# A fused attention and gated linear unit on one core: the order of all tasks from a table, squares and mean in one VectorE step

## The chip, the cores and the metric

The kernel runs on one core of a Trainium2 chip. A core has several engines, each with its own queue of instructions, which it works off in order: TensorE (PE in the profile) multiplies matrices, VectorE (DVE), ScalarE (ACT) and GpSimd (POOL) work on elements, and SyncE (SP) issues the transfers (DMA). The engines wait for each other by semaphores. Matrices are multiplied out of the on-chip memory SBUF into PSUM, which has eight banks of 128 x 512 float32.

The metric is the device time of one execution in microseconds, lower is better. The kernel before takes 272.04 us (median of three runs, 271.98 to 272.32).

## The reference

Attention with a feature map and no softmax (4 batches, 4 heads, 1088 positions, 32 wide), and behind it a normalised gated linear unit on the 4352 rows of 128:

```python
def phi(x):                                   # S1, S2: 8 x 32
    a = einsum('rd,bhsd->bhsr', S1, x); b = einsum('rd,bhsd->bhsr', S2, x)
    return einsum('bhsi,bhsj->bhsij', a, b).reshape(..., 64)
kv = einsum('bhsf,bhsd->bhfd', phi(k), v);  z = phi(k).sum(over s)
x  = (phi(q) @ kv) / (phi(q) . z + 1e-06)     # then heads side by side: 4352 x 128

xn  = x / sqrt(mean(x * x, -1) + 1e-06) * rms_g
out = (silu(xn @ w_gate) * (xn @ w_val)) @ w_out     # 128 -> 1536 -> 128
```

S1, S2 and the weights come as float64.

## The kernel before

**Attention.** For each batch, `kside` loads the transposed keys (`kt`) and the values (`vt`), multiplies the keys by S1 and S2 (L570, result in a PSUM bank), makes the 64 products per head (`product`, L531 on DVE or L513 on POOL, into `phi`), and sums `phi` times values over the positions (L580) into `kv`. The 4352 queries are worked in nine chunks, eight of 512 and one of 256. For chunks 0 and 1, `qside` makes the products in natural layout (L624, L531, `phn`) and transposes them (L632). For the others it multiplies first (L651, `sab`), stores the halves to memory (`far`) and reads them back spread out (`at`, `bt`); L677 multiplies them. Then come the numerator and denominator (L693), the division (L711, L712, L703), the squares (L715 on ACT, with the sum over the row written by the same instruction's accumulator), mean plus epsilon (L725 on DVE), the power of -1/2 (L728 on POOL), `xn` (L731 or L749), its transposes (L735), and `x_hi` and `x_lo`.

**Weights.** The float64 words of one of 12 slices of the weights, `w_raw` (384 KB), are turned into float32 on DVE in five steps of 128 x 384 (L426 or, on ACT, L445; L429, L433, L437, L440), then split into a high part `w_hi` (ACT, L494) and the rest `w_lo` (L497, DVE or POOL).

**The gated unit.** A slot is one chunk with one slice, 108 in all. Its gate goes to a bank `g_ps` and its value to a bank `v_ps`, each with three matmuls in a fast format, high by high, high by low, low by high (L786). ACT takes the silu (`s`, L795), DVE multiplies (`h`, L798), ACT rounds it to `h_hi` (L813), DVE takes the rest `h_lo` (L816), and three more matmuls add to the chunk's output in `o_ps` (L822). The first four and the last two slots use one float32 matmul instead (L805). There are two banks each of `g_ps` and `v_ps`, one `o_ps`, three `att`; four buffers of `h` and five each of `h_hi` and `h_lo`. The slots of chunks 0 and 1 are taken in halves of six slices, so that each slice of the weights serves two chunks.

**What sets the order.** None of this is issued where it stands in the code. Each step is given to a planner (`Plan.add`) as a task with its possible engines and their lengths, what it reads and writes, and its buffers. `Plan.forward` then walks a model of the engines: among the tasks that could start, it takes the one with the smallest `late`, a due time out of a table with one number per task (`LATE`), decides the engine by which would end first, and emits the instructions sorted by the modelled start. Where the model shows PE idle, small matmuls on zeros are put in (`keep_warm`, L420), the fillers. The instruction order on each engine is then fixed by dependencies.

Of the kernel before, what the change touches and what calls it, by code (L numbers as in the profile page):

```python
# [912 lines left out]
```

## Time and profile before

| what | value |
|---|---|
| median of the runs | 272.04 us |
| the profiled execution | 272.2 us |
| its span, first to last instruction | 270.0 us |
| PE busy | 263.7 us (98%) |
| DVE busy | 201.0 us (74%) |
| ACT busy | 162.1 us (60%) |
| POOL busy | 23.2 us (9%) |
| read from memory, written | 18.69 MB, 3.08 MB |

The span is shorter than the execution's time by what lies before the first and behind the last instruction. In rows of the order of time the columns are start, length, engine, line, operation, output and inputs with shapes and count, and in brackets the idle time before and what ended it. Lengths of successive instructions on one engine overlap, so that the cost of one in a stream is the distance from its start to the next. In rows of groups they are the sum of the lengths and the mean in ns, then the engine's idle time ahead of the group. Plain float32 matmuls appear as two instructions each. In rows by stretch they are the busy time of PE, the weight load, DVE, ACT and POOL, then the granted clock of TensorE, the share of the transfer engines, and GB/s.

### The profile page before, as it was taken

The page shows a single profiled execution, that of the slowest core. Times are in us where ns is not written, and L with a number is a line of the kernel's source. Part 1 is how long each engine was busy: PE and PEld are TensorE (multiplying, and loading weights), DVE is VectorE, ACT ScalarE, POOL GpSimd, SP SyncE. Part 2 cuts the span into 40 slices and gives each one's busy share as a digit, 9 for nine tenths or more (in the row PEclk, how much of TensorE's full clock was granted, in tenths as well). Part 3 has the DMA queues.
Part 4 walks back from the last instruction along what each step waited for, and adds up shares of the span by engine and source line. Part 5 has one row for each costly group of instructions (what it writes and reads, how often), then busy time and mean ns, then how long its engine had stood idle before and what let it go on. Part 6 is the DMA issues. An engine that isn't in the chain of part 4 may idle for free.

```text
span 270.0 us, 4975 instructions
## 1 busy us (share of the span) xinstructions
PE 263.7 (98%) x1842; PEld 209.4 (78%) x1842; DVE 201.0 (74%) x383; ACT 162.1 (60%) x385; POOL 23.2 (9%) x37
## 2 busy tenths in 40 slices
PE   7899999999999999999999999999999999999995
PEld 4767687687788787778778787887777887887895
DVE  3799999999676786659646967678757755967582
ACT  4488796557554665717587556546646553855671
POOL 3132221230100010000100010001000100000000
PEclk9999999999999999999999999999999999999999
DMA  6999333041045001520016101610042001200100
GB/s 201 395 401 353 105 92 83 0 128 55 2 123 170 4 0 47 129 79 2 0 58 161 35 1 40 165 34 0 10 131 75 0 0 50 81 0 0 41 0 19
DMA packets 12087, 22.08 MB, mean 82 GB/s; under 512 B 1568, under 2 KB 3360, under 8 KB 12064
## 3 DMA queue, kind: packets, MB, share of 16 engines
q1 hardware_dynamic: 11920, 21.78, 25.5%
q8 instruction: 14, 0.23, 0.3%
q14 instruction: 9, 0.07, 0.1%
q10 hardware_dynamic: 144, 0.00, 0.0%
HBM read 18.69 MB, written 3.08 MB: 81 GB/s over the span
## 4 chain that ended last, share of the span: by engine, by line
PE 90%; DVE 4%; DMA 2%; ACT 1%; SPq 1%; issue 1%; POOL 0%; ACTq 0%
PE g_ps L786 26%; PE v_ps L786 26%; PE o_ps L822 24%; PE att L693 3%; PE att L580 3%; DMA vt<-v 2%; PE o_ps L805 2%; PE att L735 1%; PE att L651 1%; PE att L570 1%; PE o_ps L580 1%; DVE h L798 1%; DVE w_tmp L433 1%; DVE h_lo L816 0%; ACT h_hi L813 0%
## 5 line engine op out<-in xcount | busy, mean ns | idle before, releaser
L798 DVE TENSOR_TENSOR h<-v_ps,s 128x512 f32<-128x512 f32 (+2 forms) x109 | 70.1, 654 | 32.8 <-ACT s L795 16.1
L795 ACT ACTIVATE s<-g_ps 128x512 f32<-128x512 f32 (+1 forms) x108 | 60.2, 572 | 38.9 <-PE g_ps L786 21.6
L813 ACT CAST h_hi<-h 128x512 fp32r<-128x512 f32 (+1 forms) x102 | 59.5, 598 | 27.1 <-DVE h L798 23.0
L816 DVE TENSOR_TENSOR h_lo<-h,h_hi 128x512 fp32r<-128x512 f32 (+1 forms) x102 | 66.3, 667 | 10.4 <-ACT h_hi L813 9.0
L786 PE MATMUL g_ps<-x_hi,w_hi 128*128 128x512 f32 (+2 forms) x111 | 43.2, 389 | 0.0
L786 PE MATMUL v_ps<-x_hi,w_hi 128*128 128x512 f32 (+2 forms) x111 | 42.7, 384 | 0.0
L786 PE MATMUL g_ps<-x_hi,w_lo 128*128 128x512 f32 (+2 forms) x111 | 41.9, 378 | 0.4 <-DVE w_lo L497 0.4
L786 PE MATMUL v_ps<-x_lo,w_hi 128*128 128x512 f32 (+2 forms) x111 | 42.0, 378 | 0.0
L786 PE MATMUL v_ps<-x_hi,w_lo 128*128 128x512 f32 (+2 forms) x111 | 41.8, 377 | 0.0
L786 PE MATMUL g_ps<-x_lo,w_hi 128*128 128x512 f32 (+2 forms) x111 | 41.8, 378 | 0.0
L822 PE MATMUL o_ps<-h_hi,w_hi 128*128 128x512 f32 (+1 forms) x102 | 40.1, 393 | 0.0
L822 PE MATMUL o_ps<-h_lo,w_hi 128*128 128x512 f32 (+1 forms) x102 | 39.1, 383 | 0.0
L822 PE MATMUL o_ps<-h_hi,w_lo 128*128 128x512 f32 (+1 forms) x102 | 39.1, 383 | 0.0
L728 POOL TENSOR_TENSOR rstd<-ms,mhalf 128x4 f32<-128x4 f32 (+1 forms) x10 | 10.0, 1000 | 187.6 <-DVE ms L725 187.6
L786 PEld LDWEIGHTS g_ps<-x_hi,w_hi 128*128 128x128 f32 x111 | 20.9, 188 | 5.3 <-ACT s L795 0.6
L786 PEld LDWEIGHTS v_ps<-x_hi,w_hi 128*128 128x128 f32 x111 | 20.9, 188 | 4.6 <-DVE h L798 0.3
L786 PEld LDWEIGHTS g_ps<-x_hi,w_lo 128*128 128x128 f32 x111 | 20.9, 188 | 4.4 <-DVE w_lo L497 0.8
L786 PEld LDWEIGHTS v_ps<-x_lo,w_hi 128*128 128x128 f32 x111 | 20.9, 188 | 4.2
L786 PEld LDWEIGHTS g_ps<-x_lo,w_hi 128*128 128x128 f32 x111 | 20.8, 188 | 4.2
L786 PEld LDWEIGHTS v_ps<-x_hi,w_lo 128*128 128x128 f32 x111 | 20.9, 188 | 3.9
L822 PEld LDWEIGHTS o_ps<-h_hi,w_hi 128*128 128x128 f32 x102 | 19.2, 188 | 5.5 <-issue 1.3
L822 PEld LDWEIGHTS o_ps<-h_lo,w_hi 128*128 128x128 f32 x102 | 19.2, 188 | 4.1
(85 smaller groups left out, 257.8 us busy)
## 6 DMA issues: line engine op xcount, KB each, us to landing
w_raw<-w SPq DMA_DIRECT2D x12, 384.0 KB
bt<-far SPq DMA_DIRECT2D x24, 128.0 KB
at<-far SPq DMA_DIRECT2D x12, 256.0 KB
q<-qT SPq DMA_DIRECT2D x8, 256.0 KB
outT<-o_sb SPq DMA_DIRECT2D x8, 256.0 KB
vt<-v SPq DMA_DIRECT2D x4, 340.0 KB
kt<-kT SPq DMA_DIRECT2D x4, 320.0 KB
vt<-v SPq DMA_DIRECT2D x4, 272.0 KB
```

The source lines that it names most:

```text
L433: nc.vector.tensor_scalar(out=u, in0=u, scalar1=5, scalar2=2, op0=ALU.logical_shift_left, op1=ALU.logical_shift_right)
L570: nc.tensor.matmul(out=ab()[hf * HALF:(hf + 1) * HALF, (t - lo) * HALF:(t - lo + 1) * HALF], lhsT=kt()[:, s0:s0 + HALF], rhs=sblk, start=T ...
L580: nc.tensor.matmul(out=kvv[rows, h // 2, :], lhsT=phi()[:, t, h * F:(h + 1) * F], rhs=vt()[:, t, h, :], start=(t == 0 and h < 2), stop=(t ...
L693: nc.tensor.matmul(out=nv[hf * HALF:(hf + 1) * HALF, t, p, :], lhsT=phi()[:, p, l0:l0 + HALF], rhs=kvs[(s0 + l0) // S][:, p, :], start=Tru ...
L728: nc.gpsimd.tensor_tensor(out=rstd()[:, us, 0], in0=ms()[:, us], in1=mhalf[:, us], op=ALU.pow)
L786: nc.tensor.matmul(out=acc()[:, cs], lhsT=wt[:, j, i3, :], rhs=x()[:, cs], start=(i == 0), stop=(i == 2))
L795: act(n, lambda: nc.scalar.activation(out=s()[:, :n], in_=gps()[:, :n], func=AF.Silu), cols(gps, whole[0]), [s])
L798: cs.stop - cs.start, lambda cs=cs: nc.vector.tensor_tensor(out=h()[:, cs], in0=vps()[:, cs], in1=s()[:, cs], op=ALU.mult),
L805: (cs.stop - cs.start) * 1.69, lambda cs=cs: nc.tensor.matmul(out=o_ps()[:, cs], lhsT=w_f[:, j, 2], rhs=h()[:, cs], start=first, stop=last ...
L813: act(n, lambda: nc.scalar.copy(out=h_hi()[:, :n], in_=h()[:, :n]), hs, [h_hi], True)
L816: eng.tensor_tensor(out=h_lo()[:, :n], in0=h()[:, :n], in1=h_hi().bitcast(F32)[:, :n], op=ALU.subtract)
L822: nc.tensor.matmul(out=o_ps()[:, :n], lhsT=wt[:, j, 2, :], rhs=x()[:, :n], start=first and i == 0, stop=last and i == 2,)
```

## The change

**The order.** `LATE` and the planner's choice are replaced by two tables: `ORDER`, the list of all 1252 tasks in the order in which they are placed, and `ON`, one letter for each task that has more than one possible engine. `Plan.follow` only computes modelled starts along that list, for the fillers and for the order in which instructions of different engines are emitted.

**Engines.** More tasks have a choice: the 64 products of keys and natural queries and those of the other chunks (`phi`, `phn`, `phiq`) on DVE or POOL, `h_lo` on DVE or POOL, plain copies on ACT or DVE. By the table, 48 of 102 `h_lo`, seven `phiq` and four `phi` or `phn` now are POOL's, and DVE has four output copies that were ACT's. The copy ahead of a product now takes both factors, not one.

**The norm.** The squares leave ACT: one DVE instruction multiplies, scales by 1/128, adds up and adds epsilon; L715 and L725 go, and L588 comes, 34 times, each with its accumulator read. The norm's weights come as a last column of batch 0's keys, in place of a transfer of their own on ACT's queue; ACT copies the column (L415).

**Loads.** The first slice of the weights is loaded first, the first queries in two halves, and batch 0's values in three pieces.

```diff
-LATE = """
--37035 -1206 -8314 1298 -10490 18870 15192 16396 -27501 -26844 -12692 -5713 -5435 -16853 4745 -3012 -1650 -18178 12804 -4772 -6470 -36037 -1883 12817
...
+ORDER = """
+67 68 69 70 11 0 12 1 4 2 3 5 6 39 40 8 34 16 71 66 72 20 35 9 41 13 205 21 7 22 210 73 77 17 36 42 14 18 211 24 15 28 75 25 206 297 74 37 207 212 26
...
+ON = (
+    "apadadaddaapaadaaadppappadpappappaddapdadpdppadpaddadpadddadddapaadaaddaapaddddaapdadddpdpadddddddppddpddddadadapdadddpp"
...
+    def follow(self, clock0, filler):
...
+            t.on = {"a": "act", "d": "dve", "p": "pool"}[next(many)] if len(t.ways) > 1 else next(iter(t.ways))
+        for i in map(int, ORDER.split()):
+            t = self.tasks[i]
...
     def product(out, ab, m, writes):
+        both = sb("both", [P, 4 * H, 2, R], 3)
...
+        copy(m * HALF, lambda: both()[:, :m * H], view, [ab], [both])
+        plan.add({
+            "dve": on_dve(m * H * F, lambda: outer(nc.vector, view())),
+            "pool": on_pool(m * H * F * 0.85, lambda: outer(nc.gpsimd, both()[:, :m * H]), PHI_POOL),
+        }, [ab, both], writes)
...
-            cs = slice(lo * P, hi * P)
+            cs = slice(lo * P, hi * P + (first and hi == KT))
...
+            act(1, lambda: nc.scalar.copy(out=gain_t, in_=kt()[:, SP:]), [(kt, 1)], ["gain"], True)
...
-                plan.add({"act": Way(300, 400, lambda t=t, u=u, sq=sq: nc.scalar.activation(
-                    out=sq()[:, t], in_=x()[:, u + t], func=AF.Square, accum_out=ss()[:, u + t:u + t + 1]
-                ))}, [(x, u)], [(sq, t), (ss, u + t)])
+                def mean(t=t, u=u, sq=sq):
+                    nc.vector.tensor_tensor_reduce(
+                        out=sq()[:, t], in0=x()[:, u + t], in1=x()[:, u + t], scale=1.0 / DM, scalar=EPS, op0=ALU.mult, op1=ALU.add,
+                        accum_out=ms()[:, u + t:u + t + 1],
+                    )
+
+                plan.add({"dve": Way(265, 345, mean, True)}, [(x, u)], [(sq, t), (ms, u + t)])
...
-            dve(n, lambda: low(nc.vector), [*hs, h_hi], [h_lo], lock=True)
+            plan.add({
+                "dve": on_dve(n, lambda: low(nc.vector), True), "pool": on_pool(n, lambda: low(nc.gpsimd), H_POOL)
+            }, [*hs, h_hi], [h_lo])
...
-    kT = np.zeros((B, H * D, SP), np.float32)
+    kT = np.zeros((B, H * D, SP + 1), np.float32)
...
+    kT[0, :, SP] = moe_rms_g
```

**Three places in the order.** The first is PE between the sums of batch 0 and the first gate matmul; `phn` and `phiq` are the queries' features, `xn` the normalised rows, and the rows with `const` are fillers. Before:

```order
L580 MATMUL o_ps<-vt,phi 64x34 x12
L420 MATMUL att<-const-float32-0.0 1x128
L693 MATMUL att<-kv_73,phiq 64x66 x16
L420 MATMUL att<-const-float32-0.0 1x128 x11
L735 MATMUL att<-ident,xn 128x128 x2
```

Now, with the numbers of the tiles, since rows read alike without:

```order
L449 MATMUL o_ps_228<-vt_114,phi_174 64x34 x36
L566 MATMUL att_279<-kv0_73,phiq_226 64x66 x8
L566 MATMUL att_289<-kv0_73,phiq_226 64x66 x8
L502 MATMUL att_304<-ident_66,phn_202 128x128 x4
L520 MATMUL att_318<-q_159,sab_88 64x256 x2
L502 MATMUL att_331<-ident_66,phn_202 128x128 x4
L566 MATMUL att_341<-kv0_73,phiq_321 64x66 x8
L608 MATMUL att_359<-ident_66,xn_350 128x128 x2
L566 MATMUL att_367<-kv0_73,phiq_321 64x66 x8
L658 MATMUL v_ps_385<-x_hi_376,w_hi_90 128x256
```

The transposes and sums of chunk 1 (`phn_202`, `phiq_321`) and the first product of chunk 2 (`q_159`) now stand where fillers stood; before, they came behind the first gate matmuls.

The second is PE at the sums of batch 1. Before, again with numbers:

```order
L580 MATMUL att_802<-vt_134,phi_793 64x34 x12
L570 MATMUL att_821<-sblk_88,kt_303 64x64 x6
L570 MATMUL att_829<-sblk_88,kt_303 64x64 x6
L786 MATMUL g_ps_838<-x_hi_339,w_hi_91 128x512
L786 MATMUL g_ps_838<-x_hi_339,w_lo_92 128x512
```

Now:

```order
L658 MATMUL v_ps<-x_lo,w_hi 128x512
L449 MATMUL att_707<-vt_407,phi_561 64x34 x12
L520 MATMUL att_727<-q_603,sab_88 64x256 x2
L449 MATMUL att_707<-vt_407,phi_561 64x34 x24
L520 MATMUL att_767<-q_517,sab_88 64x256 x2
L658 MATMUL g_ps_773<-x_hi_581,w_hi_90 128x512
```

Before, the other 24 sums followed nine gate and value matmuls later; now all 36 and the first products of two chunks stand together.

The third is DVE behind the first division, and POOL in the stage in which the weights are converted. DVE before:

```order
L703 TENSOR_TENSOR x_291<-att_251,rden_276 128x256
L711 TENSOR_SCALAR den_294<-att_263 128x8
L712 RECIPROCAL rden_299<-den_294 128x8
L703 TENSOR_TENSOR x_291<-att_263,rden_299 128x256
L725 TENSOR_SCALAR ms_305<-ss_297 128x2
```

DVE now:

```order
L575 TENSOR_TENSOR x_309<-att_279,rden_302 128x256
L583 TENSOR_SCALAR den_313<-att_289 128x8
L588 ISA sq_315,ms_316<-x_309 128x128
L588 ISA ms_316 128x1
L588 ISA sq_315,ms_316<-x_309 128x128
L588 ISA ms_316 128x1
L584 RECIPROCAL rden_324<-den_313 128x8
```

POOL now, where before only `w_lo` and `rstd` stood:

```order
L381 TENSOR_TENSOR w_lo_91<-w_f_89,w_hi_90 128x256 x2
L688 TENSOR_TENSOR h_lo_839<-h_677,h_hi_799 128x512
L381 TENSOR_TENSOR w_lo_91<-w_f_89,w_hi_90 128x128
L688 TENSOR_TENSOR h_lo_900<-h_837,h_hi_880 128x512
L546 TENSOR_TENSOR phiq_878<-at_725,bt_765 128x512
```

`ISA` is the new instruction, printed as its multiply and its accumulator read. The squares come between the first half's division and the second's, and POOL takes `h_lo` and `phiq` in turn with `w_lo`.

More of the change, by code (lines that the diff above doesn't have):

```diff
@@ L138, in __init__ @@
         self.at, self.ways, self.deps, self.bufs, self.due = at, ways, deps, bufs, due
-        self.next, self.late, self.start, self.on, self.end = [], 0.0, None, None, None
+        self.next, self.late, self.start, self.on, self.end, self.only = [], 0.0, None, None, None, None
 class Plan:
@@ L204, in backward @@
-    def backward(self, lead, each):
-        for t in reversed(self.sorted()):
-            w = min(t.ways.values(), key=lambda w: w.occ + w.against)
-            e = next(k for k, v in t.ways.items() if v is w)
-            late = 1e9 if t.due is None else FIRST + each * t.due
-            for s in t.next:
-                to = next(iter(s.ways))
-                late = min(late, s.late - (w.occ if e == to == "pe" else lead * (w.lat + self.hop(e, to) + (FLIGHT + SETTLE if e == "dma" else 0))))
-            t.late = late
@@ L251, in ready @@
             for b in t.bufs:
-                if b.live:
-                    continue
-                before = b.row[:b.at]
-                if before and not before[-1].live:
-                    return None
-                held = sum(o.left > 0 for o in before[-3 * b.bufs:])
-                if held >= b.bufs:
-                    return None
-                if b.at >= b.bufs:
-                    done = sorted((o.until for o in before if not o.left), reverse=True)
-                    at = max(at, done[b.bufs - 1 - held] + HOP[e])
+                if b not in opened:
+                    opened[b] = [len(b.tasks), 0]
+                    row = free[id(b.row)]
+                    row.sort()
+                    at = max(at, row.pop(0) + HOP[e])
@@ L298, in forward @@
+            if e == "pe" and at - clock[e] > GAP:
                 k = int((at - clock[e] - SPARE) / UNIT)
@@ L351, in run, with attention_then_glu @@
                 filler(x)
-        return best
+        return end, out, {t: (t.on, t.start, t.end, t.late) for t in self.tasks}
 @with_exitstack
-def attention_then_glu(ctx, tc, kT, v, qT, sw, w, gain, out):
+def attention_then_glu(ctx, tc, kT, v, qT, sw, w, out):
     nc = tc.nc
@@ L368, in ps, with gate, pe @@
         return plan.buf(psum, [P, 512], F32, name, bufs)
-    def pe(ns, emit, reads, writes, due=None, exact=True):
-        return plan.add({"pe": Way(ns, ns + 165, emit, exact=exact)}, reads, writes, due)
+    def gate(i):
+        return ps("g_ps", GBANKS) if GBANKS < 4 else ps(("g_ps", "v_ps")[i], 2)
+    def pe(ns, emit, reads, writes, due=None, tiled=True):
+        return plan.add({"pe": Way(ns, ns + 165, emit, tiled=tiled)}, reads, writes, due)
     def on_act(n, emit, sbuf=False, against=0):
@@ L561, in kside @@
         for i, (lo, hi) in enumerate(groups):
-            m, ab = hi - lo, ps(("g_ps", "v_ps")[i % 2], 2) if first else ps("att", 3)
+            m, ab = hi - lo, gate(i % 2) if first or b == 1 and KEY1 else ps("att", ATT)
             if not i:
-                acc = ps("o_ps", 1) if first else ps("att", 3)
+                acc = ps("o_ps", 1) if first else ps("att", ATT)
             def mm(lo=lo, hi=hi, ab=ab):
                 for t in range(lo, hi):
-                    for hf in range(2):
-                        s0 = t * P + hf * HALF
+                    for rows in range(HALF), range(HALF, P):
+                        s0, n0 = t * P + rows.start, rows.start
                         nc.tensor.matmul(
-                            out=ab()[hf * HALF:(hf + 1) * HALF, (t - lo) * HALF:(t - lo + 1) * HALF],
-                            lhsT=kt()[:, s0:s0 + HALF], rhs=sblk, start=True, stop=True,
+                            out=ab()[n0:rows.stop, (t - lo) * HALF:(t - lo + 1) * HALF],
+                            lhsT=kt()[:, s0:s0 + len(rows)], rhs=sblk, start=True, stop=True,
                         )
@@ L583, in kvmm @@
                         )
-            pe(118 * m + 60, mm, [*of(kt, KPIECES, lo, hi), "sblk"], [ab])
-            product(lambda lo=lo, hi=hi: phi()[:, lo:hi], ab, m, [(phi, i)], first and i in POOL_K)
-            pe(232 * m + 60, kvmm, [(phi, i), *of(vt, VPIECES, lo, hi)], [acc])
+            pe(116 * m, mm, [*of(kt, KPIECES, lo, hi), "sblk"], [ab])
+            product(lambda lo=lo, hi=hi: phi()[:, lo:hi], ab, m, [(phi, i)])
+            pe(232 * m, kvmm, [(phi, i), *of(vt, vpieces, lo, hi)], [acc])
         for hh in range(2):
@@ L616, in qside @@
             for u in range(0, nt, 2):
-                ab = ps("att", 3)
-                tr = ps(("g_ps", "v_ps")[u // 2], 2) if first else ps("att", 3)
+                ab = ps("att", ATT)
+                tr = gate(u // 2) if first else ps("att", ATT)
                 def abmm(u=u, ab=ab):
@@ L774, in slot @@
         up, rest_of = halves if t < 2 or not left else whole, halves if not left else whole
-        gps, vps = ps("g_ps", 2), ps("v_ps", 2)
+        gps, vps = gate(0), gate(1)
         s, h = sb("s", [P, 512], 2), sb("h", [P, 512], 4)
@@ L804, in slot @@
                 pe(
-                    (cs.stop - cs.start) * 1.69, lambda cs=cs: nc.tensor.matmul(
+                    (cs.stop - cs.start) * 1.676 + 4, lambda cs=cs: nc.tensor.matmul(
                         out=o_ps()[:, cs], lhsT=w_f[:, j, 2], rhs=h()[:, cs], start=first, stop=last and cs.stop == n
                     ),
-                    [("w_f", j)] + cols(h, cs), [*cols(o_ps, cs), (o_ps, "group")], due,
+                    [("w_f", j)] + cols(h, cs), [*cols(o_ps, cs), (o_ps, "group")], due, False,
                 )
@@ L824, in down @@
                     )
-            pe(n * 1.365, down, [h_hi, h_lo, ("w_hi", j, 1), ("w_lo", j, 1)], cols(o_ps, whole[0]), due, False)
+            pe(r3(n), down, [h_hi, h_lo, ("w_hi", j, 1), ("w_lo", j, 1)], cols(o_ps, whole[0]), due, False)
         if not last:
@@ L831, in slot @@
             part = parts[c] = sb("part", [P, 512], 2)
-            act(n, lambda: nc.scalar.copy(out=part()[:, :n], in_=o_ps()[:, :n]), done, [part])
+            copy(n, lambda: part()[:, :n], lambda: o_ps()[:, :n], done, [part])
             return
@@ L841, in slot @@
         else:
-            act(n, lambda: nc.scalar.copy(out=o_sb()[:, :n], in_=o_ps()[:, :n]), done, cols(o_sb, whole[0]))
+            copy(n, lambda: o_sb()[:, :n], lambda: o_ps()[:, :n], done, cols(o_sb, whole[0]))
         load(n * P * 4, lambda: nc.sync.dma_start(out=out[:, s0:s0 + n], in_=o_sb()[:, :n]), [("out", c)], cols(o_sb, whole[0]))
```

271 lines of the change are left out of this document (83 added, 188 removed), and 81 rows, old and new, of tables (LATE, ORDER).

## The prediction

> **What bounds the kernel now.** I read the page's busy line and its chain first, then the order of time on PE, then the waits, then the groups by form.
>
> ```profile
> span 270.0 us, 4975 instructions
> PE 263.7 (98%) x1842; PEld 209.4 (78%) x1842; DVE 201.0 (74%) x383; ACT 162.1 (60%) x385; POOL 23.2 (9%) x37
> PE 90%; DVE 4%; DMA 2%; ACT 1%; SPq 1%; issue 1%; POOL 0%; ACTq 0%
> ```
>
> PE is 98% busy and carries 90% of the chain that ended last. A gain must therefore come from PE time that is no work: fillers and waits, and whatever a matmul costs beyond its stream. The profiled execution took 272.2 us, 2.2 more than its span; the median of the three runs is 272.04. I sum against 272.2 and take 0.2 off at the end.
>
> The start, from PE in order of time:
>
> ```profile
> 11.77 1.16 PE L693 MATMUL att<-kv,phiq 128*64 128x66 f32 x32 [0.27 <-ACT kv L595]
> 12.85 2.60 PE L420 MATMUL att<-const-float32-0.0 128*1 128x128 f32 x22
> 15.76 0.62 PE L735 MATMUL att<-ident,xn 128*128 128x128 f32 x2 [0.30 <-ACT xn L749]
> 17.05 0.62 PE L735 MATMUL att<-ident,xn 128*128 128x128 f32 x2 [0.35 <-ACT xn L749]
> 18.03 0.39 PE L786 MATMUL v_ps<-x_hi,w_hi 128*128 128x256 f32 x1
> 50.87 0.50 PE L786 MATMUL g_ps<-x_hi,w_hi 128*128 128x512 f32 x1
> 51.81 0.50 PE L786 MATMUL g_ps<-x_hi,w_lo 128*128 128x512 f32 x1 [0.45 <-DVE w_lo L497]
> 266.04 1.04 PE L805 MATMUL o_ps<-h,w_f 128*128 128x256 f32 x6
> ```
>
> The first gate matmul starts at 18.03. The work before it (L570, L624, L580, L632, L693, L735), by the distance from one start to the next, adds up to about 7.5 us, so PE is 10.5 us behind its own work there. After it I find one real wait: the matmul of 50.87 streams 0.23, and its successor starts at 51.81, about 0.7 late, for a `w_lo` of DVE. PE is then 11.2 behind and stays so; the last matmuls start at 266.04.
>
> DVE is the cause of that wait. In the weight stage it has no air:
>
> ```profile
> 30.00:40.00 10.00, 10.00 (x57) 7.83 (x56) 9.79 (x22) 9.04 (x22) 2.25 (x3) 1.00 0.47 124
> 40.00:50.00 10.00, 10.00 (x44) 7.90 (x43) 9.93 (x19) 7.17 (x16) 1.73 (x2) 1.00 0.22 61
> 220.00:250.00 30.00, 30.00 (x147) 23.89 (x146) 21.17 (x36) 18.79 (x38) 0.64 (x1) 1.00 0.09 30
> ```
>
> The columns are PE, PEld, DVE, ACT, POOL. From 30 to 50 us DVE works 19.7 of 20 us and PE 20 of 20. Later DVE has 9 us in 30 to spare. So there are three places: the start, the weight stage to about 57 us, and the long rest, where only PE's own cost counts.
>
> **The change part by part.** *1. Fewer changes of shape on PE.* The matmuls of the attention use half the columns of the array (128*64), those of the GLU all. What a change between them costs stands in these rows:
>
> ```profile
> 62.75 0.40 PE L786 MATMUL g_ps<-x_lo,w_hi 128*128 128x512 f32 x1
> 63.08 1.16 PE L693 MATMUL att<-kv,phiq 128*64 128x66 f32 x32
> 64.17 0.50 PE L786 MATMUL g_ps<-x_hi,w_hi 128*128 128x512 f32 x1
> 64.50 0.39 PE L786 MATMUL g_ps<-x_hi,w_lo 128*128 128x512 f32 x1
> 64.74 0.39 PE L786 MATMUL g_ps<-x_lo,w_hi 128*128 128x512 f32 x1
> 251.32 0.39 PE L822 MATMUL o_ps<-h_lo,w_hi 128*128 128x512 f32 x1
> 251.55 0.38 PE L735 MATMUL att<-ident,xn 128*128 128x128 f32 x2
> 251.68 0.48 PE L822 MATMUL o_ps<-h_hi,w_hi 128*128 128x512 f32 x1
> 252.00 0.39 PE L822 MATMUL o_ps<-h_hi,w_lo 128*128 128x512 f32 x1
> ```
>
> A wide matmul lasts 0.24 to the next start (64.50 to 64.74). It is 0.33 to the narrow group (62.75 to 63.08), and 0.33 for the first wide one behind it (64.17 to 64.50): 0.1 us for each change. A pair of full-width transposes (251.32 to 252.00, 0.68 with two matmuls of 0.23) costs its own 0.22 and no change. The table gathers the narrow groups, as the second place of the order shows: one stretch with two edges where there were two stretches with four. Over both whole orders, fillers aside, I count 56 changes between narrow and wide before and 34 now: 22 x 0.1 = **2.2 us less** on the bound engine. The other matmuls are the same 1413; fillers go from 21 to 13. Bounds: 0, if a change is hidden where it now falls, to 2.6 (26 x 0.1, those behind the first gate matmul alone, 48 to 22).
>
> *2. The start.* Weights are now loaded first, so `s_raw` comes behind 512 KB.
>
> ```profile
> 3.78 0.23 DVE L472 TENSOR_TENSOR sblk<-s_tmp,s_top 128x64 uint32<-128x64 uint32 x1
> 9.48 0.36 DVE L426 TENSOR_SCALAR w_tmp<-w_raw 128x384 uint32<-128x384 uint32 x1 [0.60 <-DMA w_raw<-w]
> 15.30 0.56 DVE L440 SCALAR_TENSOR_TENSOR w_f<-w_raw,w_tmp 128x384 uint32<-128x384 uint32 x1
> 3.50:4.00 0.50, 0.50 (x4) 0.26 (x2) 0.47 (x4) 0.00 (x0) 0.00 (x0) 1.00 1.03 376
> ```
>
> At 0.35 to 0.38 MB/us the extra 0.52 MB take 1.4 to 1.9 us (more with its short rows), so `sblk`, done at 4.01 before, comes at about 5.9. In return the first conversion ends near 7 instead of 11.8. On PE, as the first place shows, work of chunks 1 and 2 fills what fillers held: 16 more sums (1.0), eight transposes (0.9), one `sab` product (0.5) and four small ones (0.3), less two transposes of `xn` that now come later: about 10.2 us of work, edges included, ahead of the first gate matmul. When does that start? I walk DVE's and PE's rows on from `sblk` with the lengths of before. The narrow products of queries and keys run from 6.2 to 8.3; the first `phn` on DVE ends at 7.75 and the first `phi` at 8.9, which frees the bank for the last keys (9.5); the second transposes of chunk 0 end at 10.1. `phn` has one buffer, so DVE's `phn` of chunk 1 starts only then, and two `phi` follow to 12.3. Three conversion steps stand ahead of DVE's `kv` copy (13.9), ACT's waits for it, and the sums of L566 start at about 14.1, where L693 started at 11.77. From there to the first gate matmul it was 6.3 us (11.77 to 18.03), of which 1.3 for the second pair of transposes (15.76 to 17.05), which now stands behind the first gate matmuls. So 14.1 and 5.0: about 19. What is queued behind the later `kv` copy on DVE is the second slice's conversion and the division, and PE fills that time with chunk 1's transposes. So PE is 8.8 behind its work there instead of 10.5, but the second halves of `x_hi` and `x_lo`, queued on DVE behind eight square instructions, cost it some 0.8 again. The lead is about 1 us, and it lasts only if the weight stage lets it.
>
> *3. Squares to DVE, and `h_lo` in part to POOL.* The third place shows both. Prices:
>
> ```profile
> L798 DVE TENSOR_TENSOR h<-v_ps,s 128x512 f32<-128x512 f32 x96 | 65.4, 689 | 29.4 <-PE v_ps L786 14.9 <-ACT s L795 13.2
> L816 DVE TENSOR_TENSOR h_lo<-h,h_hi 128x512 fp32r<-128x512 f32 x92 | 62.5, 694 | 10.2 <-ACT h_hi L813 9.0
> L715 ACT ACTIVATION_READ_ACCUMULATOR sq<-x 128x1 f32 x34 | 6.4, 187 | 0.0
> L497 DVE TENSOR_TENSOR w_lo<-w_f,w_hi 128x128 fp32r<-128x128 f32 x3 | 0.9, 287 | 0.0
> L440 DVE SCALAR_TENSOR_TENSOR w_f<-w_raw,w_tmp 128x384 uint32<-128x384 uint32 x12 | 7.2, 596 | 0.1
> L433 DVE TENSOR_SCALAR w_tmp<-w_tmp 128x384 uint32<-128x384 uint32 x12 | 4.6, 390 | 0.2
> L497 POOL TENSOR_TENSOR w_lo<-w_f,w_hi 128x256 fp32r<-128x256 f32 x7 | 5.3, 753 | 9.2 <-ACT w_hi L494 9.2
> L513 POOL TENSOR_TENSOR phi<-both 128x768 f32<-128x768 f32 x1 | 1.5, 1507 | 3.5 <-ACT bs L528 3.5
> 16.56 0.96 DVE L437 SCALAR_TENSOR_TENSOR w_tmp<-w_raw,w_tmp 128x384 uint32<-128x384 uint32 x1
> 16.39 0.72 POOL L497 TENSOR_TENSOR w_lo<-w_f,w_hi 128x256 fp32r<-128x256 f32 x1
> 38.36 1.01 DVE L816 TENSOR_TENSOR h_lo<-h,h_hi 128x512 fp32r<-128x512 f32 x1
> 55.27 0.82 DVE L440 SCALAR_TENSOR_TENSOR w_f<-w_raw,w_tmp 128x384 uint32<-128x384 uint32 x1
> ```
>
> A square has no row. Nearest are DVE's 128x128 (287 ns, some 0.2 to the next start) and ACT's accumulator read (187, some 0.1): 0.3 a pair, bounds 0.2 and 0.47 (both at full length). POOL's 128x512 lies between its 256 and 768 rows: 1.13 us.
>
> Counting both DVE orders at 0.09 less than these lengths (successive rows overlap): before, the `w_lo` that stalled PE (slice 8) is row 122 of DVE's order with 42.9 us of work (44 conversion steps 18.3, 12 `h` and 8 `h_lo` 12.4), against 39.8 us of PE work ahead of its use: DVE 3.1 behind. Now the tightest is slice 7: 135 rows, about 46.4 us with squares at 0.3, against 44.6 on PE: 1.8 behind. That gives PE **1.3 us**, as far as DVE is dense. Its own start adds about **0.4**: the second slice's conversion ended at 15.86 with 9.5 us of work done, 6.4 behind; by the walk it ends at 14.45 with 8.5 done, 5.95 behind.
>
> Against it stands POOL. While POOL runs `w_lo` at 16.39, DVE's two-input step at 16.56 takes 0.96 instead of its 0.56. Five such steps, the first at 38.36 and the last at 55.27, are 1.8 us longer together than their kind, during 6.3 us of POOL's work between 30 and 57 us. POOL now has about 11.4 us there (`phiq`, `h_lo` among ten `w_lo`), so 3.2: **1.4 us more**, bounds 0 and 5. [...]
>
> *4. At nothing.* The small load of the gain on ACT's queue goes (an ACT copy instead, with ACT 60% busy). From 57 us on, 42 of 48 `h_lo` on POOL at 1.13 need a chain of about 3.6 us behind their two gate groups; the order leaves at least 4.6 us of PE work there, save in the last 20 us, where tiles are half as long. A bank of `v_ps` is reused after no less than 1.05 us of PE work in both orders. If that cover were short, each place would cost a few tenths. The end (last copy and store, 2.9 us behind the last matmul) is the same.
>
> Sum: -2.2 -1.3 -0.4 +1.4 = -2.5: 269.7 in the profiled execution, **269.5** by the median.
>
> **Rivals.** *Second:* DVE doesn't bind any more, and the lead of the start is kept: 1.7 less 0.8 at the start, the 0.7 of 51 us, and the 2.2: about 3.8 less, 268.2; 267.3 without the 0.8. For it speaks that 23 us of POOL is all it did before, so it has room; against it DVE's 9.9 of 10. *Third, slower:* POOL's instructions hold DVE in the weight stage, at its conversion steps between 25 and 57 us. If each of some 15 costs half its 1.13, DVE loses 8.5 instead of 1.8: +6.7 -2.2 -1.7, 274.8. It decides from 5.7 us of lost DVE time on. Against: only 1.8 of 6.3 us was lost before. *Fourth:* a square costs 0.47 or more: eight stand ahead of the decisive `w_lo`, +1.4: 270.9. [...] *Fifth:* the changes of shape were hidden or reappear: 271.7, which is close to no change.
>
> **How the numbers follow.** Forecast 0.42, second 0.25, third 0.13, fourth 0.12, fifth 0.08. The forecast's own range, from its bounds, is 267.3 to 271.0 (squares at 0.2 or 0.47 change it by -0.8 or +1.4, no loss to POOL by -1.4). The range for 8 in 10 reaches from the second rival's low end, 266.7, to 272.2. A measurement here tells 0.2% (0.54 us). Faster: 0.41 + 0.24 + 0.09 + 0.02 = 0.76; within: 0.11; slower: 0.13, the third.
>
> **What would show it.** The first gate matmul near 19, with six or more microseconds of attention work ahead of it that stood later; twelve or thirteen fewer isolated narrow groups, each edge 0.1; DVE at 9.8 in 30 to 50 us and PE's waits there on `w_lo`; squares near 0.3 a pair; `h_lo` on POOL near 1.13 and DVE's two-input steps stretched beside it; PE without waits from 65 to 245. It is wrong if PE waits more than 3 us between 20 and 60, or in the long rest, or if the groups' edges cost nothing.

## The result

| | before | after |
|---|---|---|
| median of the runs | 272.08 us (271.98 to 272.32) | 268.05 us (266.87 to 268.88) |
| ratio | | 0.985 (0.983 to 0.987) |
| profiled execution, its span | 272.2, 270.0 | 267.74, 266.0 |
| first gate matmul on PE | 18.03 | 20.78 |
| from there to the end of the span | 252.0 | 245.2 |
| last matmuls on PE start | 266.04 | 261.90 |

The change saves 4.0 us, 1.5%. The forecast was 269.5 with a range of 266.7 to 272.2. One later execution of the changed kernel, in the run "after, again" below, took 508.67 us for a cause that no profile shows, and is left out of every figure here.

### The profile page after: what moved, and what is told of

Read it like the earlier page. It is cut to its first block, busy times and chain, and to the rows that moved or that the text cites. A ratio compares the mean times of both kernels' runs of the same rounds, so it can differ in the third digit from the quotient of the medians.

```text
span 266.0 us, 4946 instructions
## 1 busy us (share of the span) xinstructions
PE 258.9 (97%) x1826; PEld 208.7 (78%) x1826; DVE 184.3 (69%) x396; ACT 147.3 (55%) x315; POOL 94.9 (36%) x94
## 4 chain that ended last, share of the span: by engine, by line
PE 89%; DVE 5%; ACT 2%; DMA 1%; issue 1%; POOL 0%; DVEq 0%; ACTq 0%
PE g_ps L658 26%; PE v_ps L658 26%; PE o_ps L696 24%; PE att L566 3%; PE att L449 2%; PE o_ps L677 2%; PE att L608 2%; PE att L439 1%; DMA w_raw<-w 1%; DVE h L670 1%; PE att L520 1%; DVE w_lo L381 1%; PE att L502 1%; ACT phiq L275 1%; ACT both L275 1%
## 5 line engine op out<-in xcount | busy, mean ns | idle before, releaser
L688 POOL TENSOR_TENSOR h_lo<-h,h_hi 128x512 fp32r<-128x512 f32 (+1 forms) x48 | 60.8, 1276 | 104.5 <-ACT h_hi L685 86.8
L685 ACT CAST h_hi<-h 128x512 fp32r<-128x512 f32 (+1 forms) x102 | 58.7, 597 | 27.2 <-DVE h L670 21.4
L688 DVE TENSOR_TENSOR h_lo<-h,h_hi 128x512 fp32r<-128x512 f32 (+1 forms) x54 | 41.4, 781 | 10.4 <-ACT h_hi L685 10.2
L658 PE MATMUL v_ps<-x_hi,w_hi 128*128 128x512 f32 (+2 forms) x111 | 43.4, 391 | 0.2 <-DVE h L670 0.2
```

The source lines that it names most:

```text
L658: nc.tensor.matmul(out=acc()[:, cs], lhsT=wt[:, j, i3, :], rhs=x()[:, cs], start=(i == 0), stop=(i == 2))
L685: act(n, lambda: nc.scalar.copy(out=h_hi()[:, :n], in_=h()[:, :n]), hs, [h_hi], True)
L688: eng.tensor_tensor(out=h_lo()[:, :n], in0=h()[:, :n], in1=h_hi().bitcast(F32)[:, :n], op=ALU.subtract)
```

## The profile after

The page's span, busy line and chain:

```profile
span 266.0 us, 4946 instructions
PE 258.9 (97%) x1826; PEld 208.7 (78%) x1826; DVE 184.3 (69%) x396; ACT 147.3 (55%) x315; POOL 94.9 (36%) x94
PE 89%; DVE 5%; ACT 2%; DMA 1%; issue 1%; POOL 0%; DVEq 0%; ACTq 0%
```

PE in order of time: the start, the one wait behind it that a row shows, and the last matmuls.

```profile
14.82 2.03 PE L566 MATMUL att<-kv,phiq 128*64 128x66 f32 x32 [1.30 <-ACT kv L464]
16.78 1.12 PE L502 MATMUL att<-ident,phn 128*128 128x128 f32 x4
20.78 0.39 PE L658 MATMUL v_ps<-x_hi,w_hi 128*128 128x256 f32 x1
59.41 0.50 PE L658 MATMUL v_ps<-x_hi,w_hi 128*128 128x512 f32 x1 [0.20 <-DVE h L670]
261.90 1.04 PE L677 MATMUL o_ps<-h,w_f 128*128 128x256 f32 x6
```

By stretch (PE, weight load, DVE, ACT, POOL, then granted clock):

```profile
10.00:20.00 10.00, 7.75 (x135) 6.24 (x134) 7.44 (x27) 5.05 (x14) 3.50 (x5) 0.83 0.65 250
30.00:40.00 10.00, 10.00 (x53) 7.47 (x52) 9.49 (x20) 7.45 (x19) 2.71 (x6) 1.00 0.96 256
40.00:50.00 10.00, 10.00 (x109) 7.75 (x108) 9.59 (x21) 5.96 (x12) 2.83 (x4) 1.00 0.81 268
```

The first gate matmul comes 2.75 later than before, and all the rest is 6.8 shorter. DVE is nearly as full as before from 30 to 50 us (19.1 of 20 against 19.7), and yet PE hardly waits. New is the clock: 0.83 between 10 and 20 us. Sums of the same kind and number took 1.16 before (11.77) and take 2.03 here.

The work moved ahead of the first gate is 2.4 us by the lengths that the prediction used (16 sums, six transposes, four products of keys, two of queries). So 4.4 of the 6.8 is a real gain behind the first gate, and the start won nothing: PE is 10.5 us behind its own work at the first gate before, and 10.9 now (20.78 less 7.5 and 2.4). This 0.4 is what lies between the 4.4 and the 4.0 by which the span is shorter.

Where the 4.4 comes from shows in a place like this one, a chunk's transposes. Before, they stood right ahead of the narrow product of a later chunk:

```profile
72.64 0.60 PE L735 MATMUL att<-ident,xn 128*128 128x128 f32 x4
73.17 0.65 PE L651 MATMUL att<-q,sab 128*64 128x256 f32 x4
73.75 0.50 PE L822 MATMUL o_ps<-h_hi,w_hi 128*128 128x512 f32 x1
74.09 0.39 PE L822 MATMUL o_ps<-h_hi,w_lo 128*128 128x512 f32 x1
```

Now they stand alone between wide matmuls:

```profile
74.21 0.60 PE L608 MATMUL att<-ident,xn 128*128 128x128 f32 x4
74.56 0.48 PE L658 MATMUL g_ps<-x_hi,w_hi 128*128 128x512 f32 x1
74.88 0.39 PE L658 MATMUL g_ps<-x_hi,w_lo 128*128 128x512 f32 x1
```

The two rows of transposes hold the same work, but the distance to the next start is 0.53 where a narrow product follows and 0.35 where a wide matmul follows: the change from transpose to narrow costs 0.18, and the change to wide only the 0.09 by which 74.56 to 74.88 exceeds 0.23. A narrow row also ends dearer ahead of a wide matmul: the product takes 0.58 at 73.17 and 0.43 to 0.49 where another narrow group follows it.

Summed over all rows behind the first gate, as distance to the next start less 0.2325 for each 512-wide matmul: wide rows ahead of a narrow one exceed by 1.32 before (14 times) and 0.94 after (10); wide rows behind a narrow one by 2.40 (23 times) and 1.16 (11); those behind transposes by 0.09 (once) and 0.77 (nine times). Transposes' rows fall from 4.87 to 2.77, of which six moved ahead are 0.66; narrow rows from 23.20 to 19.54, of which 1.76 moved ahead. That is 0.38 + 1.24 - 0.68 + 1.44 + 1.90 = 4.3 us for the changes of shape. Rows in which a wide matmul waits between wide ones go from 0.7 to 0.6.

## The experiments

A yardstick runs through all of them: the first gate matmul's start and the time from there to the end of the span, in the profiled execution.

| kernel | median, us | span | first gate | from there |
|---|---|---|---|---|
| before | 272.08 | 270.0 | 18.03 | 252.0 |
| after | 268.05 | 266.0 | 20.78 | 245.2 |
| after, again | 267.54 | 265.6 | 20.53 | 245.1 |
| fillers in the gaps | 267.38 | 265.7 | 20.63 | 245.1 |
| kv copy first | 267.36 | 266.6 | 21.03 | 245.6 |
| both | 267.44 | 265.0 | 20.00 | 245.0 |
| groups split | 277.27 | 276.0 | 22.22 | 253.8 |
| all `h_lo` on DVE | 270.07 | 267.3 | 20.25 | 247.1 |
| squares on ACT | 269.88 | 268.1 | 22.31 | 245.8 |
| before, no fillers | 273.62 | 271.5 | 18.42 | 253.1 |
| before, gathered | 272.07 | 269.6 | 17.54 | 252.1 |
| chain of chunk 0 first | 270.32 | 268.6 | 19.54 | 249.1 |
| `s_raw` first | 268.78 | 266.4 | 21.44 | 245.0 |
| POOL's stage work on DVE | 269.95 | 266.4 | 20.09 | 246.3 |

In the variants of the changed kernel the engines' orders are issued from a fixed list; in the first run it is the unchanged one.

### Again, and the gaps of the start

> The changed kernel once more, with every engine's order as it is, beside the next three. Both theories: 266.9 to 268.9 us, as in its four runs. The gap theory expects the clock of TensorE at half for about 3 us between 14 and 18 us in most executions, and the shorter time in those where it is not.

> One filler ahead of each of the third and fourth groups of key sums and five ahead of the first query sums, in the three gaps of 0.43, 0.46 and 1.30 us in which PE waits at 11 to 14.8 us. Gap theory (the gaps lower the clock, and what is won at the start is kept, because PE waits nowhere later): clock 1.00 from 10 to 20 us, the first query sums 1.1 instead of 2.0 us, the first gate matmul near 19.4 instead of 20.8, the time 1.3 less: 266.7, with less spread. Rival (DVE's conversions and w_lo set the pace of the weight stage, the lead is given back there): first gate near 19.4, but PE waits of 1 us or more on w_lo or w_hi between 40 and 60 us, 267.8 to 268.1. Second rival (the dip has nothing to do with the gaps): clock still 0.83 in 10 to 20 us, 268.

```diff
             def kvmm(...):
+                if first and lo > 1:
+                    fill(1)
 ...
             def nmm(...):
+                if first and not u:
+                    fill(5)
```

The unchanged kernel ran at a clock of 1.00 in its profiled execution this time:

```profile
13.35 0.89 PE L449 MATMUL o_ps<-vt,phi 128*64 128x34 f32 x24 [0.46 <-DVE phi L396]
15.54 1.16 PE L566 MATMUL att<-kv,phiq 128*64 128x66 f32 x32 [1.29 <-ACT kv L464]
10.00:20.00 10.00, 7.61 (x146) 5.78 (x144) 7.78 (x27) 5.72 (x17) 3.70 (x5) 1.00 0.71 259
```

The same three gaps, but the sums take 1.16. So the gaps permit the dip, they don't force it. The kernel's first product waited for `q` and came 0.8 later than in the first profile; that ate what the clock gave.

With the fillers, the ratio to before is 0.983 (0.981 to 0.984), without them in the run beside it 0.984 (0.982 to 0.985): no measurable gain in the median, and the first gate at 20.63 where 19.4 was expected, but four executions from 267.09 to 267.62. Over the executions of the changed start without fillers (after, again, kv copy first: 13) seven have a mean granted clock of 0.994 or less and average 268.3, six are above and average 267.1. With fillers (this and the run with both, nine executions) none is below 0.998, and the average is 267.3. So about half of the executions have the dip, and they are 1.2 us longer.

### The kv copy first

> No fillers; the one DVE copy of kv of batch 0 goes ahead of the three conversion steps of weight slice 1 that stand before it (13.04 to 14.31 us). The gap ahead of the first query sums falls from 1.30 to about 0.6. Gap theory: start 0.7 earlier, and a shorter or no dip of the clock, 266.1 to 267.4. Rival (DVE's conversions set the pace): slice 1 is 0.5 later, and the time stays at 268 or gets longer, with PE waiting on w_hi of slice 1 or on w_lo later.

```diff
 phi <- v_ps, both        (DVE's order)
+kv <- o_ps
 w_tmp, w_tmp, w_tmp      (slice 1)
-kv <- o_ps
 w_f
```

> Both: the kv copy first, and fillers in what is left of the gaps (1, 1 and 2). Gap theory: clock 1.00, first gate matmul near 18.7, 266.0. Rival (DVE sets the pace of the weight stage): 267.8 to 268.1, as with the fillers alone.

The sums come 0.7 sooner, but the first gate matmul doesn't. With both edits it stands at 20.00, 13.71 behind the first product (6.29); in the unchanged kernel it is 13.69 behind it (20.53 and 6.84). The conversions, now behind the copy, push back the division, and PE stands where the bank of the sums is still held:

```profile
16.70 0.94 PE L527 MATMUL att<-q,sab 128*64 128x256 f32 x4 [0.68 <-PE att L509]
```

DVE's division of the first half reads that bank until 16.60; it begins 1.5 us behind the sums' start, against 0.7 in the unchanged kernel. A gap filled at one place of the start reopens at the next one. The 0.6 by which that execution is shorter comes from an earlier `q`, and it arrives whole at the end: from the first gate on it is 245.0 to 245.1 in these three, and 245.6 in the run with the copy alone, where PE waits 0.3 twice, for `h` and for `phi`. The rival, by which the weight stage takes a lead back, is out.

### The groups split

> The changed kernel with its gathered narrow groups taken apart again: 18 of the wide groups that follow them on PE are put between them, so that there are 18 more stretches of narrow matmuls (36 more changes of shape), with the same matmuls; other engines keep their orders. Price as the prediction put it (0.1 us a change): 3.6 us more, 245.1 to 248.7 from the first gate matmul to the end, about 271.2 us in all. Price as the rows behind the first gate of both traces give it (0.1 on entering a narrow stretch, 0.1 in its last row and 0.1 in the first wide row behind it): 18 x 0.3 = 5.4 more, 250.5, about 273. Rival (the changes were hidden, the gain came from elsewhere): 245.1 and 267.6.

```diff
 att_891 <- kv1, phiq     (PE's order, one place of several)
-att_904 <- kv1, phiq
 o_ps <- h_hi,w_hi / h_hi,w_lo / h_lo,w_hi
+att_909 <- kv1, phiq
```

The same 32 sums, apart in the split kernel:

```profile
60.59 0.69 PE L566 MATMUL att<-kv,phiq 128*64 128x66 f32 x16
61.21 0.50 PE L696 MATMUL o_ps<-h_hi,w_hi 128*128 128x512 f32 x1
61.55 0.39 PE L696 MATMUL o_ps<-h_hi,w_lo 128*128 128x512 f32 x1
```

and together in the unchanged one:

```profile
56.68 1.16 PE L566 MATMUL att<-kv,phiq 128*64 128x66 f32 x32
57.77 0.51 PE L696 MATMUL o_ps<-h_hi,w_hi 128*128 128x512 f32 x1
58.12 0.39 PE L696 MATMUL o_ps<-h_hi,w_lo 128*128 128x512 f32 x1
```

Half of the sums takes 0.62, all of them 1.09, so a second stretch costs 0.15 in the narrow row; and 61.21 to 61.55 is 0.34 again, 0.1 too long. Over the whole trace, against the unchanged kernel: 17 more stretches behind the first gate (18 were planned); wide rows ahead 2.50 against 0.94, wide rows behind 2.95 against 1.17, narrow rows 22.22 against 19.53. That is 6.0 us, 0.355 for each stretch. The other 2.7 of the 8.7 are waits that the later narrow work causes, most of it one:

```profile
122.56 0.50 PE L696 MATMUL o_ps<-h_lo,w_hi 128*128 128x512 f32 x1 [1.76 <-POOL h_lo L688]
```

The price of 0.1 a change is refuted, it is nearly twice that. The rival, hidden changes, is out. The first gate, 1.7 later than in the unchanged kernel's second profile, shows a longer dip of the clock (0.70 in 10 to 20 us); the first product was not late (6.60 against 6.84).

### POOL's and the squares' part

> All 48 h_lo of POOL go to DVE at the same places of the order. Theory (POOL's help is not what the gain came from; DVE has room behind 60 us, and two of the 48 lie before): DVE about 30 us busier, PE's waits up by no more than the two h_lo before 57 us (1.4), from the first gate to the end 245.1 to 246.5, 267.6 to 269. Rival (POOL's help frees DVE where PE waits for it): more than 3 us longer, 270.6 or more, with PE's waits on w_lo, h or h_lo. Third (POOL's instructions hold DVE and that cost PE): shorter than 245.

```diff
-ON: 48 tasks h_lo "p"
+ON: the same 48 tasks "d"
```

PE's rows with a wait, from 55 to 90 us:

```profile
58.87 0.50 PE L658 MATMUL v_ps<-x_hi,w_hi 128*128 128x512 f32 x1 [0.41 <-DVE h L670]
63.54 0.50 PE L658 MATMUL g_ps<-x_hi,w_lo 128*128 128x512 f32 x1 [0.68 <-DVE w_lo L381]
88.97 0.50 PE L658 MATMUL v_ps<-x_hi,w_hi 128*128 128x512 f32 x1 [0.47 <-DVE h L670]
```

From the first gate on 2.0 us longer, between the two bounds: it lies in these three places, with 0.1 more at each for starting again, and 0.2 at 124. POOL's `h_lo` are worth 2.0 us, not through the two before 57 us alone, but as far as DVE runs behind the conversions. Behind 125 us PE shows no wait, so there the `h_lo` could be on either engine.

> Only POOL's two-input work between 35 and 57 us goes to DVE at the same places: two h_lo, two phiq and three w_lo; POOL's h_lo behind 57 us stay. Theory (POOL's help counts where DVE is full): DVE's sum in 30 to 60 us nearer to 30, PE waits there on w_lo or h by 1 to 2 us more, 246 to 247 from the first gate, 268.5 to 269.5 in all. Rival (the prediction's third case, POOL's SBUF instructions hold DVE and cost more than they take off it): less PE wait than 0.6 us there, 244.6 or less from the first gate. Third (this stage has air): 245.1 within 0.3.

```diff
-ON: h_lo x2, phiq x2, w_lo x3 before 57 us "p"
+ON: the same seven "d"
```

```profile
63.77 0.50 PE L658 MATMUL g_ps<-x_hi,w_lo 128*128 128x512 f32 x1 [1.09 <-DVE w_lo L381]
```

1.2 us longer from the first gate, by one wait: as the first theory has it. DVE's sum from 30 to 60 us is 29.0 as in the unchanged kernel, not nearer to 30, and the median of 269.95 lies above what was expected; three of the six executions have a clock of 0.987, and one at 1.00 took 269.87, which isn't explained. Seven steps of POOL keep DVE from being late. The prediction's third rival, POOL's work as a loss in this stage, is refuted.

> The 34 squares and means go from DVE to ACT's activation with accumulator (the epsilon under the root is left out, the scale does the mean). Theory (a pair costs DVE 0.2 to the next start, and DVE does not bind): from the first gate to the end 245.1 within 0.3; the first gate itself 0.5 earlier or later, 267.1 to 268.2 in all. Rival (the prediction's fourth case: the squares are dear and DVE binds in the weight stage): 1 us or more shorter behind the first gate, and DVE's sum in 20 to 60 us falls while PE does not wait less.

```diff
-nc.vector.tensor_tensor_reduce(out=sq, in0=x, in1=x, scale=1.0 / DM, scalar=EPS, ..., accum_out=ms)
+nc.scalar.activation(out=sq, in_=x, func=AF.Square, scale=DM ** -0.5, accum_out=ms)
```

The miss is at the start. On ACT the second square stands behind a copy, and the root behind it:

```profile
17.16 0.31 ACT L588 ACTIVATE sq<-x 128x128 f32<-128x128 f32 x1 [0.83 <-DVE x L575]
18.18 0.58 ACT L275 COPY phiq<-att 128x512 f32<-128x512 f32 x1 [0.62 <-PE att L502]
18.66 0.31 ACT L588 ACTIVATE sq<-x 128x128 f32<-128x128 f32 x1
19.15 0.71 POOL L600 TENSOR_TENSOR rstd<-ms,mhalf 128x2 f32<-128x2 f32 x1 [3.04 <-ACT sq L588]
```

From the first sums (15.07) to the first gate it takes 7.24 us, against 5.96 in the profile of after (14.82 to 20.78), which had the same dip of the clock (0.83 in 10 to 20 us in both): 1.3 us. From there on it is 0.6 longer, not shorter, with waits for `h` and `h_lo`. So squares on DVE are worth 1.3 us at the start, in this order, and taking them off DVE gains nothing behind it.

### The kernel before: no fillers, and gathered

> The kernel before without the 13 fillers that its planner set between 12 and 17 us; all else as it was. Gap theory (gaps on PE at this place let the clock fall for about 3 us in some executions): a clock of about 0.8 in 10 to 20 us in half of the executions or more, and these 0.5 to 1.5 us longer: 272.5 to 273.5; the others at 272.0, and the time from the first gate to the end unchanged at 252.0. Rival (no link between gaps and clock): clock 1.00 and 272.0 in every execution.

```diff
             else:
-                filler(x)
+                pass
```

All four executions have a clock of 0.994 or 0.987, and the time is 1.006 (1.004 to 1.008) of before. The dip begins 4.5 us behind the end of the last narrow sum and lasts past the first gate, so the time from there is 253.1 and not the expected 252.0:

```profile
17.50:18.00 0.50, 0.50 (x5) 0.28 (x7) 0.35 (x2) 0.47 (x3) 0.00 (x0) 0.50 1.03 397
20.00:20.50 0.50, 0.50 (x4) 0.50 (x3) 0.50 (x2) 0.00 (x0) 0.00 (x0) 0.50 1.04 411
```

So fillers that stand where PE would only wait were worth 1.6 us.

> The kernel before, with only narrow groups moved: six products of queries (128x256) that stood right behind transposes, with their copies, go to the narrow group ahead of them, the third keys' products of batches 2 and 3 stand with the other two, and the first sums of batch 2 and 3 with the other two. Squares, w_lo and h_lo stay on their engines, the start is unchanged. Counted: seven fewer exits from a narrow stretch and one fewer entry, six fewer changes from a transpose to a narrow product, six more from a transpose to a wide matmul. By the rows behind the first gate of both traces (exit 0.26, entry 0.1, transpose to narrow 0.18, transpose to wide 0.085): 7 x 0.26 + 0.1 + 6 x 0.18 - 6 x 0.085 = 2.5 less, 269.5 us. By the price in the prediction (14 changes fewer at 0.1): 1.4 less, 270.6. Rival (without POOL's and the squares' part DVE or ACT eat the gain): 271.5 or more, with more waits of PE.

```diff
 att <- ident,xn x4       (PE's order, one of six such places)
-att <- q,sab x2
 o_ps <- h_hi,w_hi
 ...
 att <- kv,phiq x16       (the group ahead of it)
+att <- q,sab x2
```

No gain: 1.000 (0.999 to 1.0005), and 252.1 from the first gate. PE's rows show both halves. Six query products moved, and five of nine transposes lost the narrow product behind them; at the sixth place (163.77) a product of keys stands behind the transposes as before, so there only the query product between the two is gone. From 100 to 200 us PE is no longer full (100.00 before):

```profile
136.85 0.60 PE L776 MATMUL att<-ident,xn 128*128 128x128 f32 x4
138.54 0.74 DVE L782 SCALAR_TENSOR_TENSOR x_lo<-att,gain_t,x_hi 128x512 fp32r<-128x512 f32 x1
138.92 0.40 PE L827 MATMUL g_ps<-x_hi,w_lo 128*128 128x512 f32 x1
139.34 0.50 PE L827 MATMUL g_ps<-x_lo,w_hi 128*128 128x512 f32 x1
100.00:200.00 100.00, 99.54 (x698) 77.66 (x697) 70.56 (x121) 57.03 (x128) 3.02 (x3) 1.00 0.18 50
```

From the transposes to the chunk's first use of `x_lo` the product had given 0.6 us of cover. Without it PE waits at 139.34 for `x_lo`, which DVE ends at 139.28, and likewise before other chunks; at 120.78 it waits 0.28 for `phi`. By rows, the changes saved about 2.0 us (wide rows behind narrow ones 0.6, transposes' rows 0.8, with 0.4 back for wide rows behind transposes, and the narrow rows' shorter work), and the new waits cost as much: 1.5 in wide rows; the rest, which only the balance gives, in narrow ones. The rival's number came, though not as an overloaded DVE (70.6 of 100 there): what is late is single steps, 0.1 to 0.3 each. The price of a change is no gain by itself; the work has to be put where the chain behind it still has cover.

### Two other starts

> The changed kernel with fillers in the gaps of the start and with the chain of chunk 0 ahead of the conversions: on DVE the kv copy, then three conversion steps, the divisions and squares of both halves, and only then slice 1's last step; on ACT the copies and xn ahead of the casts of slice 1; on POOL the two roots ahead of slice 1's w_lo; on PE four gate and value products of the first half ahead of the second transposes, and the last query sums behind them. First gate matmul expected near 18.9 (19.5 where the first q comes late) instead of 20.5. If a lead at the start is kept to the end (the last four runs on the changed kernel took 245.0 to 245.6 from there): 264 us of span, 265.7 in all. Rival (slice 1 or a later conversion is late now, and the weight stage takes the lead back): waits of PE on w_lo or w_hi between 20 and 60 us of 1 us or more, 267.0 to 267.5.

```diff
-w_tmp x3, kv, w_f, den, ..., x       (DVE)
+kv, w_tmp x3, den, rden, x, sq x2, den, rden, x, w_f, sq x2
```

A miss. The first gate comes 1.0 sooner than in the unchanged kernel, of which 0.6 are 16 sums that now stand behind it, and the second half of chunk 0 is late, queued on DVE and ACT behind steps of slices 1 and 2:

```profile
24.18 0.39 PE L670 MATMUL g_ps<-x_lo,w_hi 128*128 128x256 f32 x1 [1.38 <-DVE x_lo L626]
```

Behind the first gate it takes 4.0 us longer, 0.6 for those sums. PE's idle time between 20 and 60 us is 1.9 us, against 0.2 in the unchanged kernel; the rest of the 4.0 isn't broken down. This run has the fillers too. The rival's waits, on `w_lo` or `w_hi`, don't appear; those on `x_hi` and `x_lo` do. A lead at the first gate alone is no gain; the second half has to follow as fast.

> The changed kernel with the fillers of the second run, and with the loads of the start in the order s_raw, both q, keys, q of chunk 1, and only then weight slice 0; DVE's, ACT's and POOL's first steps follow that order, and five fillers at 4.3 us are left out. sblk is expected near 4.0 instead of 5.95, the first narrow product at 5.0 instead of 6.0 to 6.9. If the start is set by sblk and the first q (as the prediction's walk has it): first gate 1.0 to 1.5 earlier than the 20.6 with fillers alone, near 19.3, and with 245.1 from there to the end 264.4 of span, 266.1 in all. If the start is set by the later loads of values or by DVE's conversions: first gate within 0.4 of 20.6, 267 to 267.5. If a later weight slice is then late: more than 246 from the first gate to the end, and waits on w_lo between 25 and 60 us.

```diff
-w_raw 0, q, s_raw, q, kt, q          (SP)
+s_raw, q, q, kt, q, w_raw 0
```

`sblk` ends at 3.61 and PE starts at 4.33, but one step of slice 0 was put ahead of `phn` on DVE and waited for its load:

```profile
8.00 0.36 DVE L315 TENSOR_SCALAR w_tmp<-w_raw 128x384 uint32<-128x384 uint32 x1 [4.40 <-DMA w_raw<-w]
8.28 0.69 DVE L401 TENSOR_TENSOR phn<-att,both 128x512 f32<-128x512 f32 x1
```

So the run doesn't tell what a start with `sblk` at 4.0 is worth; it stays open. It does tell that the rest is 245.0 once more.

## Why the prediction was right, point by point

**The sum was right in sign and within its range, 1.5 us too slow, and three of its four terms were wrong.** Time came out as in the second rival (268.2), but not by its way: that one kept 0.9 us of lead at the start, and there was none. That the sum came so near is partly luck: a term 2.1 too small stands beside a lead that didn't come and a loss on POOL that didn't come either.

- *Changes of shape, 2.2.* The mechanism is right; this term was mis-sized. Measured 4.3. The step "0.33 to the narrow group, and 0.33 for the first wide one behind it: 0.1 for each change" left out what lies inside the narrow row: 1.09 for 32 sums in one stretch, 0.62 for 16. With that a stretch costs 0.355, and a change from transposes to a narrow product, nine of the 48 changes that the prediction counted at 0.1, costs 0.18 in the transposes' row alone. The split kernel shows the price by itself. What TensorE does in those 0.355, no row shows.
- *The start, 0.4, and a first gate near 19.* Wrong: 20.5 to 20.8, no lead. `sblk` came as forecast (5.94), but not by short rows: 0.52 MB at 0.35 to 0.38 MB/us are 1.4 to 1.5 us, and the first step on `s_raw`, on ACT, begins that much later (4.50 against 3.02); the rest is DVE, which goes on with `s_raw` at 5.03, behind three conversion steps. Short rows are slow in the trace of before: from 1 to 3 us, with 144 of its 199 packets under 2 KB, the load queue moves 0.18 MB in 39% of the transfer engines' time, 0.23 MB/us at their full time, against 0.36 from 3 to 3.5 us with 10 of 92. The 1.48 by which `s_raw` came later leaves nothing for them. The sums came at 14.82, later than the 14.1 of the walk, and the stretch behind them took 5.0 (15.54 to 20.53) only where the clock stayed up, 6.0 where it dipped.
- *DVE 1.3 nearer, POOL's holds 1.4 back.* Their sum, nothing, is right by luck: waits of wide rows 0.7 before, 0.6 after. The 0.7 of 51 us is gone, with smaller waits at 59 and 63 us in its place, so no run shows 1.3. The 1.4 is wrong: from 30 to 57 us three DVE steps are more than 0.08 us longer than the lower quartile of their kind (of those with at least three steps), 0.9 us together, and it was six and 2.1 before. The longer steps lie behind 57 us instead, 17 of them and 11.6 us together, where PE hardly waits. Each of the 20 begins while `w_lo`, `h_lo` or `phiq` runs on POOL. That POOL's and the squares' steps were needed is shown in the other direction: undone, they cost 2.0 (`h_lo`) and, at the start, 1.3 (squares).
- *A square at 0.3.* Where POOL stands aside, it is 0.20 to the next start; beside POOL it is held:

```profile
16.98 0.28 DVE L588 CUSTOM_DVE_ANT_0 sq<-x 128x128 f32<-128x128 f32 x1
17.18 0.08 DVE L588 DVE_READ_ACCUMULATOR2_ANT ms<- 128x1 f32 x1
17.18 0.29 DVE L588 CUSTOM_DVE_ANT_0 sq<-x 128x128 f32<-128x128 f32 x1
211.11 1.29 POOL L688 TENSOR_TENSOR h_lo<-h,h_hi 128x512 fp32r<-128x512 f32 x1 [7.11 <-ACT h_hi L685]
211.16 1.38 DVE L588 CUSTOM_DVE_ANT_0 sq<-x 128x128 f32<-128x128 f32 x1
L670 DVE TENSOR_TENSOR h<-v_ps,s 128x128 f32<-128x128 f32 x2 | 0.5, 282 | 0.0
L688 DVE TENSOR_TENSOR h_lo<-h,h_hi 128x512 fp32r<-128x512 f32 x50 | 39.8, 810 | 10.0 <-ACT h_hi L685 9.8
L688 POOL TENSOR_TENSOR h_lo<-h,h_hi 128x512 fp32r<-128x512 f32 x42 | 56.4, 1353 | 100.2 <-ACT h_hi L685 83.6 <-PE o_ps L696 10.9 <-PE g_ps L658 5.7
```

  At 17 us it is as long as a plain 128x128 step (0.28). The 0.47 or more of the prediction's fourth rival isn't seen here. But the mean of all 34 is 0.38: the five that begin while `w_lo`, `h_lo` or `phiq` runs on POOL take 0.47 to 1.38 and end 0.15 us behind that step's end, and none of the other 29 is over 0.29.
- *`h_lo` on POOL at 1.13.* It takes 1.35, and DVE's own mean is 0.81 now and was 0.69. Both lie behind 57 us in the main, where PE hardly waits.
- *PE without waits from 65 to 245:* right; no row there shows one. *PE's waits of more than 3 us in 20 to 60:* none.
- *Not foreseen:* the dip of the clock, 1.2 us in about half of the executions.

By the medians of all executions about 0.2 of the gain lies outside the span (2.0 before, 1.8 now). Which edit does that was not tried.

## What to carry to other kernels

Where narrow and wide matmuls alternate on a full TensorE, count the stretches and price one from start to start across its whole row, inside included, and not by the two neighbours alone. Gather only as far as the chain behind keeps its cover: in the changed kernel, where the other engines' work was placed with it, gathering was worth 4.3 us; a smaller gathering in the old order, 2.0 us by its rows, was worth nothing. To see what a lead at the start is worth, measure from a mark behind it to the end: here that time was 245.0 to 245.2 us in five profiled executions whose first gate stood anywhere from 20.00 to 21.44, and 245.6 in a sixth, where PE waited. The mark must have the same work ahead of it in both kernels, which it had not between before and after, nor in the run with chunk 0 first.
